# Attention with a gated MLP: weights normalized ahead of their transposes, the left keys of two heads in one product, gate tokens in pairs

## The chip, the cores and the metric

The kernel runs on one core of a Trainium2 chip. The metric is the device time of the whole program in microseconds (us). In the profile, PE is TensorE (matrix products; PEld its weight loads), DVE is VectorE, ACT is ScalarE, POOL is GpSimd and SP is SyncE, which issues the transfers.

## The reference

```python
q, k, v: (8, 12, 448, 64)              # batch, heads, tokens, head size
q_n = q / rms(q) * g_q;  k_n = k / rms(k) * g_k
scores = q_n @ k_n.T / 8
attn = exp(scores - max(scores));  attn = attn / (sum(attn) + 1e-9)
x = (attn @ v), heads side by side     # (8, 448, 768)
h = gelu_tanh(x @ w_in)                # w_in 768 x 1024
u, v = h[..., :512], h[..., 512:]
v_n = layernorm(v) * g_ln
v_s = w_sg @ v_n + b_sg                # w_sg 448 x 448, over the tokens
out = x + (u * v_s) @ w_out            # w_out 512 x 768
```

## The kernel before

448 is 3 x 128 + 64, so each head has three full tiles of tokens and 64 "left" tokens. The kernel works on pairs of heads, 48 in all (`i`), and on units of two pairs (`u`). Tokens are laid out so that the left tokens of the two pairs of a unit share one tile: a unit has seven score tiles, `C7 = 7`, and the middle one (`t == CM`, `CM = 3`) is shared.

Every number is carried as two half-precision parts, high and low (`h`, `l`), so that a product becomes three: high by high, high by low, low by high.

- `load_qk`, `squares`, `norms`, `split` fetch q and k, normalize them and transpose them by DMA into `qt`.
- `load_v`, `vsquares`, `vscale`, `vsplit` fetch v (three pairs at a time, tile `vr`, from a pool of two), find one power of two per batch and split v into `vh` and `vl`, of seven chunks of 64 columns.
- `scores(u)` makes for each of the seven tiles both heads' scores in a PSUM tile `s` of two banks (`ps_s` has two of them): products on TensorE (L389), the row maximum on VectorE (L392), two exponentials on ScalarE that also give the row sums (L394), then after a `yield` the split of the weights, not yet normalized, into two halves `ahl` (L397 ScalarE, L398 VectorE, 896 elements wide) and a DMA transpose into `at_all` (L403).
- `recips(i)` takes the reciprocal of the sums (GpSimd, VectorE), splits it in two (GpSimd), and spreads it over the 64 partitions of each head by 16 small products with `ident_h` (L423) into a PSUM tile; ScalarE copies that to `row` (L426).
- `pv(i)` calls `recips`, then runs 24 products of v with the transposed weights (L446): the left keys first, in 64x64 pieces, then the full chunks, 64 columns for each head side by side; it gives way (`yield`) after blocks 4 and 8. VectorE multiplies by `row` (L450), ScalarE and VectorE split the result into `xh`, `xl` (L453, L454).
- `moe(b)` is the MLP of one batch: the gate half of the first projection with tokens on the partitions (L510; left tokens L513, whose columns are halved), gelu, layer norm; the other half (L568); the gate over the tokens (L598: four accumulators `ms_`, one for each 128 columns `f`, 9 products over full token tiles and 3 over the left 64, at partitions 0 to 63 for `f` 0 and 1 and 64 to 127 for `f` 2 and 3); the product with `u` and its split (L603 to L608, on VectorE, GpSimd and ScalarE); and the second projection (L632 to L644), copied out by L648. Its accumulators come from `ps_m`, three PSUM banks.
- `weights()` decodes the MLP's weights, which arrive as double precision, in the first part of the run.

All of these are generators. The main loop goes over the pairs and takes steps from the streams `scores` (`SC = 7`), `pv` of the pair before (`SV = 4`), `weights`, and `moe` of the batch before (`M0` to `ML` steps a pair) in proportion to those numbers; the order in which they are written gives each instruction its priority. The framework's planner then sets the final order of each engine's instructions from the priorities and its own model of their times; each engine runs its instructions in that order.

Of the kernel before, what the change touches and what calls it, by code (L numbers as in the profile page):

```python
# [22 lines left out]


# [10 lines left out]
SC, SV = 7, 4  # L35
# [11 lines left out]
def kernel(  # L47
# [54 lines left out]
    ident_h = const.tile([P, P], F16, name="ident_h")  # L102
    A.activation(out=ident_h, in_=ident, func=AF.Copy)
# [180 lines left out]
    VR = {}  # L284

    def load_v(i):

        if i >= NI:  # L290
# [72 lines left out]
    def vsplit(i):  # L363
        r = R.setdefault(i, {})
        sc = VS[i // NP]["sc"]
        vh, vl = (att.tile([P, C7, D], F16, name="v" + c, bufs=NVH) for c in "hl")
        vr = VR.pop(i)
        vf = vh.rearrange("p c d -> p (c d)")
        A.activation(out=vf, in_=vr, func=AF.Copy, scale=sc)  # L369
        V.scalar_tensor_tensor(out=vl.rearrange("p c d -> p (c d)"), in0=vr, scalar=sc, in1=vf, op0=ALU.mult, op1=ALU.subtract)  # L370
        r.update(vh=vh, vl=vl)
# [3 lines left out]
    def scores(u):  # L375
# [3 lines left out]
        sums = sml.tile([P, C7, 2], F32, name="sums", bufs=2)  # L379
        U[u]["sums"] = sums  # L380
        for t in range(C7):
# [9 lines left out]
            nm = sml.tile([P, 2], F32, name="nm", bufs=6)  # L391
            V.tensor_reduce(out=nm, in_=ps[:, :, 0:S], axis=AX.X, op=ALU.max, negate=True)  # L392
            for h in range(2):
                A.activation(out=ps[:, h, 0:S], in_=ps[:, h, 0:S], func=AF.Exp, bias=nm[:, h:h + 1], accum_out=sums[:, t, h:h + 1])  # L394
            yield
            ahl = att.tile([P, 2, 2, S], F16, name="ahl", bufs=NAH)
            A.activation(out=ahl[:, 0], in_=ps[:, :, 0:S], func=AF.Copy)  # L397
            V.tensor_tensor(out=ahl[:, 1], in0=ps[:, :, 0:S], in1=ahl[:, 0], op=ALU.subtract)  # L398
# [7 lines left out]
    def recips(i):  # L406

        u, j = divmod(i, NG)
        cs = slice(0, C4) if j == 0 else slice(CM, C7)
        sums = U[u]["sums"][:, cs].rearrange("p t h -> p (t h)")  # L410
        x, y = (sml.tile([P, 2 * C4], F32, name=f"r{c}", bufs=2) for c in "xy")
        rh, rl = (sml.tile([P, 2 * C4], F16, name=f"r{c}", bufs=2) for c in "hl")
        G.tensor_scalar(out=x, in0=sums, scalar1=1e-9, scalar2=None, op0=ALU.add)  # L413
        V.reciprocal(out=y, in_=x)
        G.tensor_copy(out=rh, in_=y)  # L415
        G.tensor_tensor(out=rl, in0=y, in1=rh, op=ALU.subtract)
        ps = ps_v.tile([P, 512], F32, name="row", tag="pv")[:, 0:S]
        for n, t in enumerate(range(cs.start, cs.stop)):
            ks, o = (slice(0, P), t * P - j * S) if t != CM else ((lo, SM), (hi, 0))[j]
            for rx in (rh, rl):  # L420
                for h in range(2):
                    w = ks.stop - ks.start
                    mm(out=ps[h * HP:(h + 1) * HP, o:o + w], lhsT=rx[ks, 2 * n + h:2 * n + h + 1].broadcast_to([w, HP]),  # L423
                       rhs=ident_h[ks, ks], start=(n == 0 and rx is rh), stop=(n == CM and rx is rl), skip_group_check=True)
        row = att.tile([P, S], F32, name="row", bufs=1)
        A.activation(out=row, in_=ps, func=AF.Copy)  # L426
        return row

    XT = {}

    def pv(i):
# [3 lines left out]

        steps = [[(slice(0, P), c + h * C4) if c < CM else (slice(h * HP, (h + 1) * HP), CM) for h in range(2)]
                 for c in range(C4)]
        blocks = [(vx, n, hx) for vx, n in ((vh, 0), (vl, 0), (vh, C7)) for hx in steps]

        blocks = blocks[CM::C4] + [x for n, x in enumerate(blocks) if n % C4 != CM]  # L440
        row = recips(i)
        yield
        ps = ps_v.tile([P, 512], F32, name="pv")[:, 0:S]
        for k_, (vx, n, hx) in enumerate(blocks):
            for h, (ks, c) in enumerate(hx):
                mm(out=ps[h * HP:(h + 1) * HP], lhsT=vx[ks, c], rhs=at_all[ks, n + c, o:o + S],  # L446
                   start=(k_ == 0), stop=(k_ == len(blocks) - 1), skip_group_check=True)
            if k_ in (4, 8):
                yield
        V.tensor_tensor(out=ps, in0=ps, in1=row, op=ALU.mult)  # L450
        xh = xp.tile([P, S], F16, name="xh")
        xl = xp.tile([P, S], F16, name="xl")
        A.activation(out=xh, in_=ps, func=AF.Copy)  # L453
# [23 lines left out]
    def moe(b, early=False):  # L477
# [21 lines left out]
        for st, (t, g) in enumerate(steps):  # L499
# [20 lines left out]
            if st % 2 == 1:  # L520
# [60 lines left out]
        gl = []  # L581
# [7 lines left out]
        for f in range(FT):  # L589
            ps = ps_m.tile([P, 512], F32, name="ms_", tag="mm")  # L590
            n = 0
            for t in range(CK):
                p0, p1, o = 0, P, t * DH + f * P
                if t == CM:
                    p0 = f // 2 * HP
                    p1, o = p0 + HP, t * DH + f % 2 * P
                for vx, wx in ((vh, ws_h), (vh, ws_l), (vl, ws_h)):
                    mm(out=ps[:, 0:S], lhsT=vx[p0:p1, o:o + P], rhs=wx[p0:p1, t], start=(n == 0), stop=(n == 11))  # L598
                    n += 1
                if t == 1:  # L600
                    yield
            gt = mlp.tile([P, S], F32, name="gt", tag="gt", bufs=NOT)
            V.scalar_tensor_tensor(out=gt, in0=ps[:, 0:S], scalar=W["gw"][:, f:f + 1], in1=bb, op0=ALU.mult, op1=ALU.add)  # L603
            G.tensor_tensor(out=gt, in0=gt, in1=u[f], op=ALU.mult)  # L604
            A.activation(out=gh[:, f], in_=gt, func=AF.Copy)
            gl.append(mlp.tile([P, S], F32R, name="gl", tag="ug", bufs=5))
            G.tensor_tensor(out=gl[f], in0=gt, in1=gh[:, f].bitcast(F32), op=ALU.subtract)
            G.tensor_tensor(out=gtl[:, f, half], in0=gt[:, SM:S], in1=gh[:, f, SM:S].bitcast(F32), op=ALU.subtract)  # L608
# [183 lines left out]
```

## Time and profile before

| | |
|---|---|
| median of 3 runs | 1037.53 us (1032.77 to 1038.14) |
| the profiled execution | 1033.44 us |
| its span, first to last instruction | 1031.6 us |
| mean granted TensorE clock | 0.916 of full speed |
| moved by DMA | 155.70 MB |

A group's line gives the line of the kernel, engine, operation, what is written and read, how often, then busy us, the mean of one in ns, and the engine's idle time just before it with what ended it. A line of waits gives who waited, for whom, the total in us, how many times, and the longest. The rows of a stretch give its start and end, its length, and the busy time of PE, PEld, DVE, ACT and POOL with their instruction counts, then the granted clock, the share of the DMA engines and GB/s. For a product, `128*64` is the rows and columns of the array that it uses.

### The profile page before, as it was taken

The numbers are of one execution on the slowest core, as the hardware profiler recorded it, in microseconds if no ns is written. First come the engines' busy times: TensorE is split into PE (matmuls) and PEld (weight loads), VectorE is DVE, ScalarE is ACT, GpSimd is POOL, SyncE is SP. The second block draws the span as 40 slices with busy tenths as digits, with TensorE's granted clock in tenths as the row PEclk, the third lists the DMA queues.
The fourth block names the chain that finished last, engine by engine and source line by source line (L and its number), as shares of the span: only waits on it lengthen the run. The fifth ranks groups of instructions, "written<-read, shape, count | busy, mean of one in ns | idle before, by whom it ended". The sixth has DMA issues, their size and how long they took to land.

```text
span 1031.6 us, 16639 instructions
## 1 busy us (share of the span) xinstructions
PE 829.0 (80%) x5844; PEld 421.1 (41%) x5844; DVE 733.3 (71%) x1332; ACT 738.1 (72%) x1449; POOL 386.9 (38%) x403
## 2 busy tenths in 40 slices
PE   0243666858798997899689998999779998998798
PEld 0111222324444563346234553446324563454246
DVE  6698888999587667786677758786669666766230
ACT  3767779877868767777768767987777776877351
POOL 1468614567253505243251606341533414030021
PEclk9976687969899999999699998999889999999899
DMA  6998748776886398478886488959967676556102
GB/s 163 214 228 191 166 115 196 185 176 130 181 197 150 88 204 180 98 170 145 186 175 147 99 194 183 182 123 176 194 142 160 141 166 125 106 135 123 40 1 62
DMA packets 448004, 155.70 MB, mean 151 GB/s; under 512 B 404336, under 2 KB 441776, under 8 KB 447920
## 3 DMA queue, kind: packets, MB, share of 16 engines
q1 hardware_dynamic: 447344, 154.18, 69.0%
q8 instruction: 46, 0.75, 0.3%
q10 hardware_dynamic: 576, 0.46, 0.2%
q14 instruction: 38, 0.31, 0.1%
HBM read 43.57 MB, written 11.01 MB: 53 GB/s over the span
## 4 chain that ended last, share of the span: by engine, by line
PE 34%; DVE 21%; ACT 19%; DMA 11%; issue 8%; SPq 4%; POOL 4%; ACTq 0%; POOLq 0%; DVEq 0%
PE pv L446 6%; ACT s L394 5%; DVE ahl L398 5%; PE s L389 4%; DVE nm L392 3%; ACT ahl L397 2%; DMA vr<-in_v_dram 2%; ACT sqk L308 2%; DMA raw<-in_moe_w_in_dram 2%; DMA at<-ahl 2%; POOL qk L330 2%; DMA qt<-hl 2%; DMA qk<-in_k_dram 2%; ACT hl L334 2%; SPq L336 1%
## 5 line engine op out<-in xcount | busy, mean ns | idle before, releaser
L394 ACT ACTIVATE s<-s,nm 128x448 f32<-128x448 f32 x336 | 204.0, 607 | 109.8 <-DVE nm L392 106.8
L398 DVE TENSOR_TENSOR ahl<-s,ahl 128x896 f16<-128x896 f32 x168 | 182.1, 1085 | 100.8 <-ACT ahl L397 99.8
L389 PE MATMUL s<-qt 64*128 64x448 f16 (+1 forms) x1152 | 143.2, 390 | 110.7 <-DVE ahl L398 76.4
L392 DVE TENSOR_REDUCE nm<-s 128x2 f32<-128x896 f32 x168 | 180.8, 1082 | 40.5 <-PE s L389 40.0
L397 ACT ACTIVATE ahl<-s 128x896 f16<-128x896 f32 x168 | 153.4, 920 | 5.3 <-DMA at<-ahl 3.1
L446 PE MATMUL pv<-at,vh 128*64 128x448 f16 (+1 forms) x768 | 122.7, 398 | 16.4 <-DMA at<-ahl 7.6
L413 POOL TENSOR_SCALAR rx<-sums 128x8 f32<-128x8 f32 x48 | 13.4, 278 | 311.8 <-ACT s L394 310.4
L389 PEld LDWEIGHTS <-qt 64*128 64x128 f16 (+1 forms) x1152 | 45.3, 102 | 177.2 <-issue 135.9
L330 POOL TENSOR_TENSOR qk<-qk,ny 128x896 f32<-128x896 f32 x46 | 80.8, 1774 | 85.8 <-DVE ny L125 82.3
L335 POOL TENSOR_TENSOR hl<-qk,hl 128x896 f16<-128x896 f32 x46 | 87.7, 1917 | 55.1 <-ACT hl L334 54.5
L568 PEld LDWEIGHTS <-wi 128*128 128x128 f16 x576 | 55.9, 100 | 60.2 <-issue 14.1
L446 PEld LDWEIGHTS <-vh 128*64 128x64 f16 (+1 forms) x768 | 43.4, 117 | 84.3 <-issue 70.2
L309 DVE TENSOR_REDUCE ss<-sqk 128x14 f32<-128x896 f32 x48 | 51.8, 1080 | 29.2 <-ACT sqk L308 28.9
L394 ACT ACTIVATION_READ_ACCUMULATOR s<-s,nm 128x1 f32 x336 | 67.7, 201 | 0.0
L329 POOL TENSOR_TENSOR qk<-qk,gg 128x896 f32<-128x896 f32 x23 | 48.0, 2085 | 43.2 <-ACT sqk L308 39.3
L423 PE MATMUL row<-ident_h,rh 128*64 128x128 f16 (+1 forms) x384 | 36.7, 240 | 31.7 <-POOL rh L415 24.0
L604 POOL TENSOR_TENSOR gt<-gt,u 128x448 f32<-128x448 f32 x32 | 38.5, 1206 | 60.1 <-DVE gt L603 55.9
L446 PE MATMUL pv<-at,vl 128*64 128x448 f16 (+1 forms) x384 | 60.4, 394 | 0.0
L334 ACT ACTIVATE hl<-qk 128x896 f16<-128x896 f32 x48 | 44.9, 947 | 15.9 <-POOL qk L330 8.4
L308 ACT ACTIVATE sqk<-qk 128x896 f32<-128x896 f32 x48 | 45.6, 951 | 8.2 <-DVE ss L309 4.4
L510 PEld LDWEIGHTS <-xh 128*128 128x128 f16 x288 | 27.0, 101 | 49.2 <-issue 21.9
L369 ACT ACTIVATE vh<-vr,v_s 128x448 f16<-128x448 f32 x48 | 31.9, 668 | 19.7 <-PE pv L446 19.6
(996 smaller groups left out, 1960.8 us busy)
## 6 DMA issues: line engine op xcount, KB each, us to landing
out_dram<-ot SPq DMA_DIRECT2D x56, 192.0 KB, 2.9
vr<-in_v_dram SPq DMA_DIRECT2D x32, 192.0 KB, 3.3
raw<-in_moe_w_in_dram SPq DMA_DIRECT2D x12, 512.0 KB, 5.7
qk<-in_q_dram SPq DMA_DIRECT2D x47, 128.0 KB, 2.8
qk<-in_k_dram SPq DMA_DIRECT2D x47, 128.0 KB, 2.8
vr<-in_v_dram SPq DMA_DIRECT2D x32, 144.0 KB, 3.3
qk<-in_q_dram SPq DMA_DIRECT2D x47, 96.0 KB, 2.6
qk<-in_k_dram SPq DMA_DIRECT2D x47, 96.0 KB, 2.6
```

The source lines that it names most:

```text
L308: A.activation(out=skv, in_=U[u]["qk"][:, x].rearrange("p h c d -> p (h c) d"), func=AF.Square)
L309: V.tensor_reduce(out=SS[u][:, x], in_=skv, axis=AX.X, op=ALU.add)
L330: E.tensor_tensor(out=qk, in0=qk, in1=r["rs"][:, x * SSW:(x + 1) * SSW].unsqueeze(2).broadcast_to([P, SSW, D]), op=ALU.mult)
L334: A.activation(out=h_, in_=r["qk"][:, x], func=AF.Copy)
L335: E.tensor_tensor(out=l_, in0=r["qk"][:, x], in1=h_, op=ALU.subtract)
L389: mm(out=ps[r_, h, 0:S], lhsT=qt[hs, qx, t * P + r_.start:t * P + r_.stop], rhs=qt[hs, kx, j * S:(j + 1) * S], start=(m == 0), stop=(m == 2))
L392: V.tensor_reduce(out=nm, in_=ps[:, :, 0:S], axis=AX.X, op=ALU.max, negate=True)
L394: A.activation(out=ps[:, h, 0:S], in_=ps[:, h, 0:S], func=AF.Exp, bias=nm[:, h:h + 1], accum_out=sums[:, t, h:h + 1])
L397: A.activation(out=ahl[:, 0], in_=ps[:, :, 0:S], func=AF.Copy)
L398: V.tensor_tensor(out=ahl[:, 1], in0=ps[:, :, 0:S], in1=ahl[:, 0], op=ALU.subtract)
L446: mm(out=ps[h * HP:(h + 1) * HP], lhsT=vx[ks, c], rhs=at_all[ks, n + c, o:o + S], start=(k_ == 0), stop=(k_ == len(blocks) - 1), skip_grou ...
L568: done = mm(out=ps[:, 0:S], lhsT=ww[:, g, f * P:(f + 1) * P], rhs=xx, start=(n == 0), stop=(n == 17))
```

## The change

The reciprocal of the row sums is taken in `scores`, from each tile's own sums, and the weights are multiplied by it (and by 1024, `WSC`, to use the half-precision range) while they are split, one head at a time. `recips`, `row`, `ident_h` and the multiply in `pv` go; `xh` and `xl` take 1/1024 in. v gets an eighth chunk: the left keys of the first head lie in chunk 3 (other half zero), those of the second in chunk 4 (other half zero), so that one product of 128 columns serves both heads; the zeros are written once, into two `vr` tiles that are now allocated by hand. `pv` is one block without a `yield` inside. In `moe`, the left tokens of the first projection are one step, and the gate runs `f` in pairs (0, 2) and (1, 3) with the left tokens of both side by side.

```diff
+WSC = 2.0 ** 10
-SC, SV = 7, 4
+SC, SV = 7, 3
...
-    ident_h = const.tile([P, P], F16, name="ident_h")
-    A.activation(out=ident_h, in_=ident, func=AF.Copy)
...
+    C8 = C7 + 1
+    vr_all = [ld.tile([P, GV, C8, D], F32, name=f"vr{n}", bufs=1) for n in range(NVR)]
+    for x in vr_all:
+        G.memset(x[hi, :, CM], 0.0)
+        G.memset(x[lo, :, C4], 0.0)
...
-        vr = ld.tile([P, GV, C7, D], F32, name="vr", bufs=NVR)
+        vr = vr_all[i // GV % NVR]
...
-        vh, vl = (att.tile([P, C7, D], F16, name="v" + c, bufs=NVH) for c in "hl")
+        vh, vl = (att.tile([P, C8, D], F16, name="v" + c, bufs=NVH) for c in "hl")
...
-            nm = sml.tile([P, 2], F32, name="nm", bufs=6)
+            nm, sums = (sml.tile([P, 2], F32, name=c, bufs=6) for c in ("nm", "sums"))
             V.tensor_reduce(out=nm, in_=ps[:, :, 0:S], axis=AX.X, op=ALU.max, negate=True)
             for h in range(2):
-                A.activation(..., func=AF.Exp, bias=nm[:, h:h + 1], accum_out=sums[:, t, h:h + 1])
+                A.activation(..., func=AF.Exp, bias=nm[:, h:h + 1], accum_out=sums[:, h:h + 1])
+            rc = sml.tile([P, 2], F32, name="rc", bufs=6)
+            V.tensor_scalar(out=sums, in0=sums, scalar1=1e-9, scalar2=1.0 / WSC, op0=ALU.add, op1=ALU.mult)
+            V.reciprocal(out=rc, in_=sums)
             yield
             ahl = att.tile([P, 2, 2, S], F16, name="ahl", bufs=NAH)
-            A.activation(out=ahl[:, 0], in_=ps[:, :, 0:S], func=AF.Copy)
-            V.tensor_tensor(out=ahl[:, 1], in0=ps[:, :, 0:S], in1=ahl[:, 0], op=ALU.subtract)
+            for h in range(2):
+                A.activation(out=ahl[:, 0, h], in_=ps[:, h, 0:S], func=AF.Copy, scale=rc[:, h:h + 1])
+                V.scalar_tensor_tensor(out=ahl[:, 1, h], in0=ps[:, h, 0:S], scalar=rc[:, h:h + 1], in1=ahl[:, 0, h],
+                                       op0=ALU.mult, op1=ALU.subtract)
...
-    def recips(i):
-        ...
...
     def pv(i):
-        blocks = blocks[CM::C4] + [x for n, x in enumerate(blocks) if n % C4 != CM]
-        row = recips(i)
-        yield
-        ...
-            if k_ in (4, 8):
-                yield
-        V.tensor_tensor(out=ps, in0=ps, in1=row, op=ALU.mult)
+        parts = ((vh, 0), (vl, 0), (vh, C7))
+        for k_, (vx, n) in enumerate(parts):
+            mm(out=ps, lhsT=vx[:, CM:CM + 2].rearrange("p c d -> p (c d)"), rhs=at_all[:, n + CM, o:o + S],
+               start=(k_ == 0), stop=False, skip_group_check=True)
+        for c in range(CM):
+            for vx, n in parts:
+                for h in range(2):
+                    mm(out=ps[h * HP:(h + 1) * HP], lhsT=vx[:, c + h * (C4 + 1)], rhs=at_all[:, n + c + h * C4, o:o + S],
+                       start=False, stop=(c == CM - 1 and n == C7), skip_group_check=True)
-        A.activation(out=xh, in_=ps, func=AF.Copy)
-        V.tensor_tensor(out=xl, in0=ps, in1=xh, op=ALU.subtract)
+        A.activation(out=xh, in_=ps, func=AF.Copy, scale=1.0 / WSC)
+        V.scalar_tensor_tensor(out=xl, in0=ps, scalar=1.0 / WSC, in1=xh, op0=ALU.mult, op1=ALU.subtract)
         XT[i] = (xh, xl)
         del R[i]
+        yield
...
-            if st % 2 == 1:
+            if st % 2 == 1 and (early or t != CM or g == NP - 1):
                 yield
...
-        for f in range(FT):
-            ps = ps_m.tile([P, 512], F32, name="ms_", tag="mm")
-            ...
+        for f0 in range(2):
+            psf = {f: ps_m.tile([P, 512], F32, name="ms_", tag="mm") for f in (f0, f0 + 2)}
+            for f, ps in psf.items():
+                ...
+                yield
+            for n, (vx, wx) in enumerate(((vh, ws_h), (vh, ws_l), (vl, ws_h))):
+                for f, ps in psf.items():
+                    p0, o = f // 2 * HP, CM * DH + f0 * P
+                    mm(out=ps[:, 0:S], lhsT=vx[p0:p0 + HP, o:o + P], rhs=wx[p0:p0 + HP, CM], start=False, stop=(n == 2))
+            for f, ps in psf.items():
+                ...
             yield
```

More of the change, by code (lines that the diff above doesn't have):

```diff
@@ L292, in load_v @@
         b, g = divmod(i, NP)
-        vr = ld.tile([P, GV, C7, D], F32, name="vr", bufs=NVR)
+        vr = vr_all[i // GV % NVR]
         vp = vr.rearrange("p g c d -> p g (c d)")
         src = v[b, 2 * g:2 * (g + GV)].rearrange("(g h) (p c) d -> h p g (c d)", h=2, c=C7)
-        for h, half, s0, c0, n in ((0, lo, 0, 0, C4), (0, hi, 0, C4, CM), (1, lo, C4, C4, CM), (1, hi, CM, 0, C4)):
+        for h, half, s0, c0, n in ((0, lo, 0, 0, C4), (0, hi, 0, C4, CM), (1, lo, C4 + 1, C4, CM), (1, hi, C4, 0, C4)):
             nc.sync.dma_start(out=vp[half, :, s0 * D:(s0 + n) * D], in_=src[h][:, :, c0 * D:(c0 + n) * D])
@@ L349, in vsquares @@
             VS["part", b] = sml.tile([P, NP // GV], F32, name="vpart", bufs=2)
-        n = GV * C7 * D
+        n = GV * C8 * D
         sk = prep.tile([P, n], BF16, name="sqv", tag="t4", bufs=HLB)
@@ L378, in scores @@
         qt = U[u]["qt"]
-        sums = sml.tile([P, C7, 2], F32, name="sums", bufs=2)
-        U[u]["sums"] = sums
         for t in range(C7):
@@ L390, in scores @@
                            rhs=qt[hs, kx, j * S:(j + 1) * S], start=(m == 0), stop=(m == 2))
-            nm = sml.tile([P, 2], F32, name="nm", bufs=6)
+            nm, sums = (sml.tile([P, 2], F32, name=c, bufs=6) for c in ("nm", "sums"))
             V.tensor_reduce(out=nm, in_=ps[:, :, 0:S], axis=AX.X, op=ALU.max, negate=True)
             for h in range(2):
-                A.activation(out=ps[:, h, 0:S], in_=ps[:, h, 0:S], func=AF.Exp, bias=nm[:, h:h + 1], accum_out=sums[:, t, h:h + 1])
+                A.activation(out=ps[:, h, 0:S], in_=ps[:, h, 0:S], func=AF.Exp, bias=nm[:, h:h + 1], accum_out=sums[:, h:h + 1])
+            rc = sml.tile([P, 2], F32, name="rc", bufs=6)
+            V.tensor_scalar(out=sums, in0=sums, scalar1=1e-9, scalar2=1.0 / WSC, op0=ALU.add, op1=ALU.mult)
+            V.reciprocal(out=rc, in_=sums)
             yield
             ahl = att.tile([P, 2, 2, S], F16, name="ahl", bufs=NAH)
-            A.activation(out=ahl[:, 0], in_=ps[:, :, 0:S], func=AF.Copy)
-            V.tensor_tensor(out=ahl[:, 1], in0=ps[:, :, 0:S], in1=ahl[:, 0], op=ALU.subtract)
+            for h in range(2):
+                A.activation(out=ahl[:, 0, h], in_=ps[:, h, 0:S], func=AF.Copy, scale=rc[:, h:h + 1])
+                V.scalar_tensor_tensor(out=ahl[:, 1, h], in0=ps[:, h, 0:S], scalar=rc[:, h:h + 1], in1=ahl[:, 0, h],
+                                       op0=ALU.mult, op1=ALU.subtract)
             src = ahl.rearrange("p x h n -> p (x h n)")
@@ L404, in scores @@
             yield
-    def recips(i):
[L408 to L427, printed above, removed]
     XT = {}
@@ L580, in moe @@
         gh = mlp.tile([P, FT, S], F32R, name="gh", tag="vggh")
-        gl = []
+        gl = {}
         vh, vl = V2["vh"], V2["vl"]
@@ L588, in moe @@
         bb = W["bb"]
-        for f in range(FT):
-            ps = ps_m.tile([P, 512], F32, name="ms_", tag="mm")
[L591 to L608, printed above, removed]
@@ new lines, in moe @@
+        for f0 in range(2):
+            psf = {f: ps_m.tile([P, 512], F32, name="ms_", tag="mm") for f in (f0, f0 + 2)}
+            for f, ps in psf.items():
+                n = 0
+                for t in range(CM):
+                    o = t * DH + f * P
+                    for vx, wx in ((vh, ws_h), (vh, ws_l), (vl, ws_h)):
+                        mm(out=ps[:, 0:S], lhsT=vx[:, o:o + P], rhs=wx[:, t], start=(n == 0), stop=False)
+                        n += 1
+                yield
[4 more added lines that the diff above has]
+            for f, ps in psf.items():
+                gt = mlp.tile([P, S], F32, name="gt", tag="gt", bufs=NOT)
+                V.scalar_tensor_tensor(out=gt, in0=ps[:, 0:S], scalar=W["gw"][:, f:f + 1], in1=bb, op0=ALU.mult, op1=ALU.add)
+                G.tensor_tensor(out=gt, in0=gt, in1=u[f], op=ALU.mult)
+                A.activation(out=gh[:, f], in_=gt, func=AF.Copy)
+                gl[f] = mlp.tile([P, S], F32R, name="gl", tag="ug", bufs=5)
+                G.tensor_tensor(out=gl[f], in0=gt, in1=gh[:, f].bitcast(F32), op=ALU.subtract)
+                G.tensor_tensor(out=gtl[:, f, half], in0=gt[:, SM:S], in1=gh[:, f, SM:S].bitcast(F32), op=ALU.subtract)
```

7 lines of the change are left out of this document (removed).

## The prediction

> **What bounds the kernel now.** I read the page first, then the stretches by engine, then the chain of waits, the waits of each engine, the groups by line, and last TensorE's timeline where the change touches it.
>
> Busy time on the page:
> ```profile
> span 1031.6 us, 16639 instructions
> PE 829.0 (80%) x5844; PEld 421.1 (41%) x5844; DVE 733.3 (71%) x1332; ACT 738.1 (72%) x1449; POOL 386.9 (38%) x403
> ```
> The span cut in three, and three single stretches (us; then PE, PEld, DVE, ACT, POOL busy; granted clock; DMA):
> ```profile
> 0.00:300.00 300.00, 171.50 (x1162) 79.66 (x1163) 248.33 (x435) 217.85 (x424) 152.10 (x136) 0.82 0.78 178
> 300.00:900.00 600.00, 541.85 (x3908) 276.36 (x3905) 434.39 (x817) 454.52 (x901) 211.86 (x231) 0.95 0.73 155
> 900.00:1032.00 132.00, 115.64 (x780) 65.10 (x777) 50.53 (x82) 65.71 (x126) 22.92 (x36) 0.95 0.33 72
> ...
> 100.00:200.00 100.00, 67.00 (x425) 27.88 (x425) 87.99 (x166) 84.43 (x158) 42.85 (x37) 0.74 0.74 168
> 700.00:800.00 100.00, 83.59 (x604) 40.50 (x601) 73.89 (x136) 75.13 (x150) 32.56 (x32) 0.91 0.86 171
> 800.00:900.00 100.00, 96.43 (x714) 51.60 (x714) 66.84 (x130) 74.80 (x153) 27.25 (x37) 1.00 0.64 137
> ```
> No engine is full throughout. Up to 300 us VectorE leads (83%; 88% between 100 and 200), from 300 us on TensorE (90%). The chain of waits, whole span by engine and the 300 to 900 stretch by line:
> ```profile
> PE 34%; DVE 21%; ACT 19%; DMA 11%; issue 8%; SPq 4%; POOL 4%; ACTq 0%; POOLq 0%; DVEq 0%
> ...
> by line: PE pv L446 7.0%; ACT s L394 6.9%; issue 6.7%; DVE ahl L398 4.9%; PE s L389 4.6%; DVE nm L392 3.6%; ACT ahl L397 2.7%; ACT sqk L308 2.3%; DMA vr<-in_v_dram 2.3%; ACT hl L334 2.2%; DMA qt<-hl 2.0%; DMA at<-ahl 1.9%; PE row L423 1.5%;
> ```
> So the end is set by three engines handing work to each other. A microsecond of an engine lies on that chain with a weight of its chain share over its busy share: PE 34/80 = 0.425, DVE 21/71 = 0.296, ACT 19/72 = 0.264. I price by these weights; they assume that the mixture stays, which the rivals drop. Waits from 300 to 900 us:
> ```profile
> PE s L389 <- DVE ahl L398: 18.1, 18, 3.0
> PE row L423 <- POOL rh L415: 12.9, 7, 5.3
> ...
> DVE ahl L398 <- ACT ahl L397: 69.0, 58, 3.8
> ...
> ACT s L394 <- DVE nm L392: 69.2, 39, 6.0
> ```
> VectorE and ScalarE wait mostly for one another inside a score tile; TensorE, when it waits, waits for a score tile's subtraction or for the reciprocals.
>
> **The change part by part.** Durations by group (busy us, mean ns, idle before), then two single lines:
> ```profile
> L394 ACT ACTIVATE s<-s,nm 128x448 f32<-128x448 f32 x336 | 204.0, 607 | 109.8 <-DVE nm L392 106.8
> L398 DVE TENSOR_TENSOR ahl<-s,ahl 128x896 f16<-128x896 f32 x168 | 182.1, 1085 | 100.8 <-ACT ahl L397 99.8
> ...
> L397 ACT ACTIVATE ahl<-s 128x896 f16<-128x896 f32 x168 | 153.4, 920 | 5.3 <-DMA at<-ahl 3.1
> ...
> L394 ACT ACTIVATION_READ_ACCUMULATOR s<-s,nm 128x1 f32 x336 | 67.7, 201 | 0.0
> ...
> L607 POOL TENSOR_TENSOR gl<-gt,gh 128x448 fp32r<-128x448 f32 x32 | 36.8, 1150 | 7.9 <-ACT gh L605 7.8
> ...
> L370 DVE SCALAR_TENSOR_TENSOR vl<-vr,v_s,vh 128x448 f16<-128x448 f32 x48 | 36.6, 764 | 3.0 <-ACT vh L369 3.0
> ...
> L450 DVE TENSOR_TENSOR pv<-pv,row 128x448 f32<-128x448 f32 x48 | 30.0, 624 | 22.3 <-PE pv L446 22.0 <-PE mo__6671 L636 0.4
> ...
> L426 ACT ACTIVATE row<-row 128x448 f32<-128x448 f32 x48 | 26.0, 542 | 6.5 <-PE row L423 6.3
> ...
> L453 ACT ACTIVATE xh<-pv 128x448 f16<-128x448 f32 x48 | 25.9, 540 | 18.4 <-DVE pv L450 18.4
> ...
> L414 DVE RECIPROCAL ry<-rx 128x8 f32<-128x8 f32 x48 | 9.4, 196 | 15.8 <-POOL rx L413 15.5
> ...
> L135 DVE TENSOR_SCALAR v_x<-v_x x8: 135/144/155, 38.6 to 849.5; 128x1 f32<-128x1 f32 x8
> ...
> L603 DVE SCALAR_TENSOR_TENSOR gt<-ms__3456,gw,bb x1: 684/684/684, 343.5 to 343.5; 128x448 f32<-128x448 f32 x1
> ```
> TensorE's row products (L423), in the three stretches:
> ```profile
> 0.00:300.00 300.00, 12.11 (x192) 8.24 (x192) 0.82 0.78 178
> 300.00:900.00 600.00, 26.18 (x512) 18.00 (x512) 0.95 0.73 155
> 900.00:1032.00 132.00, 3.09 (x64) 2.12 (x64) 0.95 0.33 72
> ```
> At 16 products a head pair these are 12, 32 and 4 pairs, so 42, 112 and 14 score tiles (3.5 a pair).
>
> Its timeline (start, us; both at clock 1.0), first a run of whole products, then where forms alternate, a split `pv`, and the gate's left tokens:
> ```profile
> 654.30 0.38 PE L510 MATMUL mv__7104<-wi,xl 128*128 128x512 f16 x1
> 654.52 0.59 PE L510 MATMUL mv__7104<-wi,xh 128*128 128x512 f16 x2
> ...
> 519.67 0.39 PE L510 MATMUL mv__5655<-wi,xh 128*128 128x512 f16 x1
> 520.00 0.30 PE L513 MATMUL mv__5575<-wi,xh 128*64 128x256 f16 x1
> ...
> 337.36 0.85 PE L446 MATMUL pv<-at,vh 64*64 64x448 f16 x6
> 338.15 0.74 PE L389 MATMUL s<-qt 64*128 64x448 f16 x6
> 338.82 0.38 PE L446 MATMUL pv<-at,vh 128*64 128x448 f16 x2
> ...
> 341.41 0.35 PE L598 MATMUL ms__3456<-ws_h,vl 128*128 128x448 f16 x1
> 341.60 0.35 PE L598 MATMUL ms__3491<-ws_h,vh 128*128 128x448 f16 x1
> 341.89 0.36 PE L598 MATMUL ms__3456<-ws_h,vh 64*128 64x448 f16 x1
> ```
> A 512-wide product takes 0.22 us from start to start, 0.33 when the next has another form (rows*columns); a 448-wide one 0.19 and 0.29. A change of form costs 0.10 us.
>
> The sum for 300 to 900 us:
> 1. Row products go: 1.5% of the chain, −9.0 (bounds 0 and the whole 26.2).
> 2. TensorE's waits for `rh` go: 12.9 x 0.425 = −5.5.
> 3. The multiply by `row` and `recips`' reciprocal go from VectorE: 32 x (0.624 + 0.196) = 26.2, x 0.296 = −7.8. The copy of `row` goes from ScalarE: 32 x 0.542 = 17.3, x 0.264 = −4.6. Three GpSimd steps a pair go; off the path, counted at nothing: GpSimd is 38% busy.
> 4. `pv` in one block: if one foreign block fewer splits it, two changes, 32 x 0.2 x 0.425 = −2.7 (bounds 0 and double). The whole product of the left keys replaces a pair that ran side by side, so it frees no stream of columns: nothing.
> 5. First projection: left-token products no longer handed out two at a time; up to 12 changes a batch, 5.5 batches, 6.6 x 0.425 = −2.8 (0 if the planner still mixes them).
> 6. Gate: a batch's left tokens take 4 x (3 x 0.19 + 0.2) = 3.1 us, in pairs 2 x 0.77 = 1.5: 5.5 x 1.5 x 0.425 = −3.6. The pairs hold two of three `ps_m` buffers; the 9 products of the next accumulator (1.7 us) cover an evacuation of 0.684, and without that cover each waits 0.7.
> 7. VectorE per tile: two halves with a per-row scalar, nearest L603, 2 x 0.68 − 1.085 = +0.27, and two tiny operations, 0.144 + 0.196 = +0.34: 0.61 x 112 = 68.3, x 0.296 = +20.2. L398's own 4.9% of the chain gives 29.4 x 0.61/1.085 = 16.5. I take +18.4.
> 8. ScalarE per tile: two halves, between L453's 0.540 and L394's 0.607, taken 0.56: +0.20 x 112 x 0.264 = +5.9.
> 9. But the subtraction can begin after half a copy, 0.36 earlier, at the 58 waits of 69.0 us: 20.9 x 0.296 = −6.2 (0 if the waits are for something earlier).
> 10. Two more hand-overs a tile (sums to VectorE, reciprocal to ScalarE). No row prices one; between 0 and a tiny operation's 0.144, taken 0.1: 112 x 0.1 x 0.296 = +3.3.
> 11. `v` has eight chunks, not seven: at most 0.764 x 64/448 = 0.11 on each of VectorE and ScalarE, 32 x 0.11 x 0.56 = +2.0. `ident_h` and the zero fill of `vr` fall into the start and cost nothing while the first loads run; without that, under 1 us.
>
> Sum −12.6. The transposes on SyncE's queue become ready with the second half, some 0.3 us later, and loads queue behind them; `at<-ahl` has 1.9% of the chain, so I count it within 10.
>
> 0 to 300 us: rows 12.1 x 0.425 = −5.1, the waits for `rh`, taken as half of the later stretch's, −2.8, `pv` and gate −1. VectorE: 42 x 0.61 − 12 x 0.82 = +15.8 in a stretch where it leads; between its weight (+4.7) and all (+15.8) I take +7. Sum −1.9. 900 us on, TensorE 88% busy and mostly alone: rows −2, gate of two batches −2, VectorE +1.6, and at the end the second pair's two gate chains come together on GpSimd (one more 1.15 and its neighbour, +2): −0.4.
>
> Together −14.9 us: span 1031.6 to 1016.7. The profiled execution took 1033.4, so 1.8 lies around the span: 1018.5. The median of the runs, 1037.5, stands 4 us above that execution; I give 1018.
>
> **The rivals.**
> *Slower: VectorE's queue.* The tiny operations wait for the second exponential's sum. If one stands in VectorE's order before another tile's maximum, that maximum waits up to 0.607 + 0.201 = 0.81 us, and ScalarE (which waited 69.2 us for maxima) with it. It eats the gain from 15/0.81 = 19 of 168 tiles on; at a quarter of them, 42, it ends 34 us above the forecast, 1052. For it: VectorE at 88% between 100 and 200 us. Against: the waits now are handed between two tiles in flight, so the planner can put other work there.
>
> *TensorE was the bound alone.* Then 300 to 900 us shrinks until VectorE is the limit: 434.4 + 68.3 − 26.2 + 3.5 = 480, at the 88% of the 100 to 200 row 545 us, −55, and 975 in all. For it: 96.43 of 100 in the row from 800. Against: TensorE has only 34% of the chain.
>
> *The clock takes it back.* The row from 700 shows 83.6% busy and clock 0.91, that from 800 shows 96.4% and 1.00. TensorE after has some 542 − 26 − 13 − 8 = 495 of 587 us, 84%: at 0.91 for 0.95 its work grows by 4.4%, 21.8 x 0.425 = +9, 1027. The Trainium skill (TensorE: Matmul & The Clock Gate, Why this matters for your kernels) advises against idle gaps of over some 3 us between bursts, since the clock falls; the rows agree in direction, not in which gap does it.
>
> *No change: work only moved.* The three engines' sum from 300 to 900 us is 1430.8; after, TensorE −47, VectorE +46, ScalarE +9. At the same overlap the time stays 1033. The same if the planner does not set the pairs side by side. The Trainium skill (TensorEngine Tiling (Array Packing), PSUM Bottleneck) says packing speeds TensorE but not the evacuation of PSUM, which can become the limit.
>
> **How the numbers follow.** Forecast 0.46 (1000 to 1028), TensorE alone 0.12, clock 0.14, no change 0.09, slower 0.19. From 985 to 1043 leaves out about half of the second and half of the last, 0.16 in all. A difference of 0.5% is about what can be told here. Faster: 0.46 + 0.12 + 0.09 of the clock's = 0.67; same: 0.05 + 0.09 = 0.14; slower 0.19.
>
> **What would show it.** Right: PE's busy time near 765, DVE's near 800, no row products, shorter waits of DVE for `ahl` copies, 0.19 us between the gate's left pairs. Wrong: ScalarE's copy idle for a reciprocal for more than some 20 us in all, VectorE waiting for exponentials before a tiny operation, or a clock under 0.90 with TensorE idle as before.

## The result, and the profile after

The changed kernel takes 1168.95 us (median of 4 runs, 1168.50 to 1171.91) where the kernel before takes 1036.42 on the same chip (median of 4, 1032.77 to 1038.14): a ratio of 1.129 (95% interval 1.125 to 1.133), 133 us slower. The forecast was 1018. The profiled execution took 1171.91 us, at a mean granted clock of 0.846 where before had 0.916. One execution further down, of `halves_turn`, ran slow, at a clock of 0.645 and 1282.98 us, and is left out of what is compared.

Span and busy time of the changed kernel, from its page:
```profile
span 1170.1 us, 15089 instructions
PE 820.3 (70%) x4932; PEld 404.1 (35%) x4932; DVE 807.6 (69%) x1740; ACT 780.7 (67%) x1568; POOL 352.0 (30%) x263
```
912 products are gone, and yet every engine has a smaller share of the span than before. So no engine became full; the engines stand idle for one another more. The same three stretches (the last row ends with the longer span):
```profile
0.00:300.00 300.00, 140.23 (x769) 61.77 (x769) 231.05 (x475) 198.56 (x392) 128.74 (x97) 0.78 0.68 156
300.00:900.00 600.00, 461.14 (x2816) 225.45 (x2816) 431.18 (x951) 423.70 (x855) 174.31 (x120) 0.86 0.62 138
900.00:1170.00 270.00, 218.96 (x1348) 116.91 (x1347) 145.35 (x315) 158.41 (x323) 49.00 (x46) 0.89 0.44 97
```
From 300 to 900 us TensorE was 90% busy before and is 77% now; VectorE, at 72%, is where it was. The groups around a score tile (busy us, mean ns, idle before and its cause):
```profile
L405 DVE SCALAR_TENSOR_TENSOR ahl<-s,rc,ahl 128x448 f16<-128x448 f32 x336 | 225.5, 679 | 122.7 <-ACT ahl L404 121.2
L392 PE MATMUL s<-qt 64*128 64x448 f16 (+1 forms) x1152 | 149.8, 405 | 198.4 <-DVE ahl L405 172.9
L404 ACT ACTIVATE ahl<-s,rc 128x448 f16<-128x448 f32 x336 | 208.6, 632 | 110.8 <-DVE ahl L405 57.3
L397 ACT ACTIVATE s<-s,nm 128x448 f32<-128x448 f32 x336 | 203.5, 606 | 110.6 <-DVE nm L395 107.0
L399 DVE TENSOR_SCALAR sums<-sums 128x2 f32<-128x2 f32 x168 | 45.9, 273 | 62.3 <-ACT s L397 61.7
```
The waits over the whole span, before and then after (who waits, for whom, us, times, longest):
```profile
PE s L389 <- DVE ahl L398: 76.4, 35, 9.0
PE pv L446 <- DMA at<-ahl: 7.6, 3, 3.0
PE row L423 <- DVE xl L454: 2.7, 1, 2.7
...
DVE ahl L398 <- ACT ahl L397: 99.8, 82, 4.5
...
ACT s L394 <- DVE nm L392: 106.8, 58, 6.0
```
```profile
PE s L392 <- DVE ahl L405: 172.9, 59, 11.9
PE pv L423 <- DMA at<-ahl: 46.4, 14, 8.3
...
DVE ahl L405 <- ACT ahl L404: 121.2, 151, 3.9
DVE sums L399 <- ACT s L397: 61.7, 72, 2.2
...
ACT s L397 <- DVE nm L395: 107.0, 102, 5.3
ACT ahl L404 <- DVE ahl L405: 57.3, 64, 2.5
```
The chain of waits of this execution can be followed back only from the end to 1098 us, so the argument goes by waits and single tiles. The wait that grew most is TensorE's for a score tile's PSUM to come free: 76.4 to 172.9 us. The last line has no counterpart before: ScalarE, which copies a tile's weights, waits for VectorE, which subtracts them. One tile shows it, before and then after (start, us, engine, operation, idle before and its releaser):
```profile
960.53 0.21 ACT L394 ACTIVATION_READ_ACCUMULATOR s<-s,nm 128x1 f32 x1
960.77 0.92 ACT L397 ACTIVATE ahl<-s 128x896 f16<-128x896 f32 x1
961.72 1.09 DVE L398 TENSOR_TENSOR ahl<-s,ahl 128x896 f16<-128x896 f32 x1 [0.42 <-ACT ahl L397]
```
```profile
559.89 0.17 DVE L399 TENSOR_SCALAR sums<-sums 128x2 f32<-128x2 f32 x1 [0.96 <-ACT s L397]
560.10 0.17 DVE L400 RECIPROCAL rc<-sums 128x2 f32<-128x2 f32 x1
560.35 0.64 ACT L404 ACTIVATE ahl<-s,rc 128x448 f16<-128x448 f32 x1 [0.48 <-ACT s L397]
561.01 0.68 DVE L405 SCALAR_TENSOR_TENSOR ahl<-s,rc,ahl 128x448 f16<-128x448 f32 x1 [0.75 <-ACT ahl L404]
561.62 1.08 DVE L395 TENSOR_REDUCE nm<-s 128x2 f32<-128x896 f32 x1
561.74 0.63 ACT L404 ACTIVATE ahl<-s,rc 128x448 f16<-128x448 f32 x1 [0.75 <-DVE ahl L405]
562.61 0.68 DVE L405 SCALAR_TENSOR_TENSOR ahl<-s,rc,ahl 128x448 f16<-128x448 f32 x1
```
Before, copy and subtraction take 2.04 us from the copy's start (960.77 to 962.81). After, they go by turns: copy of head 0, subtraction of head 0, copy of head 1, subtraction of head 1. The second copy starts only when the first subtraction ends (561.69), although it reads other columns; so it does in 158 of the 168 tiles, taken in order of time. VectorE fills the pause with the next tile's maximum, and the last subtraction waits until that is done: 2.94 us (560.35 to 563.29). Two small operations and two hand-overs stand ahead of all this.

**The hold of a score tile.** There are two PSUM tiles `s`. I took, in each trace, the time from the first product of each of the 168 tiles to the end of its last subtraction (the hold) and from there to the first product of the tile that takes its place (the gap). With two tiles used in turn, half the mean of their sum is the time from one tile to the next by construction; what the table can show is which part grew:

| | hold | gap | half the sum | tile to tile, measured |
|---|---|---|---|---|
| before | 9.62 | 1.53 | 5.58 | 5.60 |
| after | 10.99 | 1.83 | 6.41 | 6.41 |

The difference, 0.83 (of the unrounded means) x 168 = 139 us, is the loss with 6 us to spare, and most of it is hold: 1.37 us more a tile, against 0.30 of gap. That the hold also sets the pace doesn't follow from the sum. In `two_psum_before` below, where TensorE is 99% busy, the same account over both heads' tiles gives 10.19 and 0.30, half the sum 5.24, and 5.27 measured. For the changed kernel it rests on TensorE's longer waits above and on the runs below, which alter what happens inside the hold. Two parts of the hold grew: from the end of the exponentials to the copy's start, 0.85 to 1.63 (1.03 to the reciprocal, 0.60 on to the copy), and from the copy's start to the last subtraction's end, 2.53 to 4.05. Two shrank, perhaps since engines were freer: products to maximum, 2.57 to 2.15, and maximum to exponential, 1.03 to 0.54.

### The profile page after: what moved, and what is told of

It is laid out like the page before. It is cut to its first block, busy times and chain, and to the rows that moved or that the text cites. A ratio compares the mean times of both kernels' runs of the same rounds, so it can differ in the third digit from the quotient of the medians.

```text
span 1170.1 us, 15089 instructions
## 1 busy us (share of the span) xinstructions
PE 820.3 (70%) x4932; PEld 404.1 (35%) x4932; DVE 807.6 (69%) x1740; ACT 780.7 (67%) x1568; POOL 352.0 (30%) x263
## 5 line engine op out<-in xcount | busy, mean ns | idle before, releaser
L405 DVE SCALAR_TENSOR_TENSOR ahl<-s,rc,ahl 128x448 f16<-128x448 f32 x336 | 225.5, 679 | 122.7 <-ACT ahl L404 121.2
L392 PE MATMUL s<-qt 64*128 64x448 f16 (+1 forms) x1152 | 149.8, 405 | 198.4 <-DVE ahl L405 172.9
L404 ACT ACTIVATE ahl<-s,rc 128x448 f16<-128x448 f32 x336 | 208.6, 632 | 110.8 <-DVE ahl L405 57.3
L428 PE MATMUL pv<-at,vh 128*64 128x448 f16 x576 | 110.1, 441 | 0.0
L399 DVE TENSOR_SCALAR sums<-sums 128x2 f32<-128x2 f32 x168 | 45.9, 273 | 62.3 <-ACT s L397 61.7
L423 PE MATMUL pv<-at,vh 128*128 128x448 f16 x96 | 42.4, 441 | 63.8 <-DMA at<-ahl 46.4
L428 PE MATMUL pv<-at,vl 128*64 128x448 f16 x288 | 63.2, 436 | 0.0
L428 PEld LDWEIGHTS <-vh 128*64 128x64 f16 x576 | 39.2, 133 | 55.6 <-issue 45.0
L433 DVE SCALAR_TENSOR_TENSOR xl<-pv,xh 128x448 f16<-128x448 f32 x48 | 29.7, 619 | 31.9 <-ACT xh L432 31.9
L432 ACT ACTIVATE xh<-pv 128x448 f16<-128x448 f32 x48 | 26.0, 542 | 32.5 <-PE pv L428 32.4
```

The costliest lines, as they stand in the source:

```text
L392: mm(out=ps[r_, h, 0:S], lhsT=qt[hs, qx, t * P + r_.start:t * P + r_.stop], rhs=qt[hs, kx, j * S:(j + 1) * S], start=(m == 0), stop=(m == 2))
L399: V.tensor_scalar(out=sums, in0=sums, scalar1=1e-9, scalar2=1.0 / WSC, op0=ALU.add, op1=ALU.mult)
L404: A.activation(out=ahl[:, 0, h], in_=ps[:, h, 0:S], func=AF.Copy, scale=rc[:, h:h + 1])
L405: V.scalar_tensor_tensor(out=ahl[:, 1, h], in0=ps[:, h, 0:S], scalar=rc[:, h:h + 1], in1=ahl[:, 0, h], op0=ALU.mult, op1=ALU.subtract)
L428: mm(out=ps[h * HP:(h + 1) * HP], lhsT=vx[:, c + h * (C4 + 1)], rhs=at_all[:, n + c + h * C4, o:o + S], start=False, stop=(c == CM - 1 and ...
```

## The experiments

Theory: the turns of the two engines on one PSUM tile, and the reciprocal ahead of the copy, lengthen the hold. Rivals: VectorE's wait for the sums alone; the clock; the rest of the change (one-block `pv`, MLP). All differences below are to the kernel before in the same set of runs, 1033.81, 1036.11, 1036.72 or 1037.20 us.

**Half the change each.** `norm_alone` is the kernel before with the weights normalized in `scores` as in the change; `pv`'s blocks, its split left keys and the MLP stay as before.
```diff
+ scores as in the change (sums, rc, scaled halves by turns)
- row = recips(i);  ps = ps * row
```


> The kernel before with one part of the change: the reciprocal of each tile's sums in scores, the weights scaled while they are split one head at a time, no row products. pv in its old blocks, gate and projection as before. Theory 1 (the two heads' halves take turns: the second copy on ScalarE stands behind the first subtraction on VectorE, and the tiny operations make VectorE wait): nearly all of the 133 us is here, 1130 to 1180 us. Rival 2 (pv in one block and the eighth chunk of v set TensorE waiting): within 20 us of before, 1020 to 1055. Rival 3 (both in equal parts): near 1100.

1164.41 us, 1.125 (1.121 to 1.130): +131.

`rest_alone` is the changed kernel with `recips`, `row` and the 896-wide copy and subtraction put back.

> The changed kernel with the old normalization put back: whole-tile copy and subtraction, reciprocals and row products after the sums of all tiles, multiply by row. pv in one block, eighth chunk of v, gate in pairs and the projection's left tokens in one step stay. Theory 1 (halves in turns): near the kernel before or a little faster, 1015 to 1045. Rival 2 (pv in one block, v's scale): 1120 to 1170. Rival 3 (both): near 1100.

1045.70 us, 1.011 (1.007 to 1.014): +12. The two add up to 143, the whole change makes 133. Nearly all of the loss comes with the normalization.

**The turns.** `halves_turn` takes the kernel before and only cuts its copy and subtraction in two, without scaling:
```diff
-            A.activation(out=ahl[:, 0], in_=ps[:, :, 0:S], func=AF.Copy)
-            V.tensor_tensor(out=ahl[:, 1], in0=ps[:, :, 0:S], in1=ahl[:, 0], op=ALU.subtract)
+            for h in range(2):
+                A.activation(out=ahl[:, 0, h], in_=ps[:, h, 0:S], func=AF.Copy)
+                V.tensor_tensor(out=ahl[:, 1, h], in0=ps[:, h, 0:S], in1=ahl[:, 0, h], op=ALU.subtract)
```


> The kernel before with one edit: copy and subtraction of a tile are split in two, copy of head 0, its subtraction, copy of head 1, its subtraction, with no scaling and no reciprocals per tile. Only the turns and the two extra instructions are added. Theory 1 (the turns cost): 1090 to 1140. Rival 1b (what costs is the tiny operations' wait for the sums): only the added busy time, 168 x 0.14 us on VectorE and 168 x 0.16 us on ScalarE, of which a third shows: 1040 to 1060.

1121.17 us, one execution and so without an interval: +87. Hold and gap are 10.43 and 1.78, 6.12 from tile to tile. Its waits:
```profile
DVE ahl L399 <- ACT ahl L398: 150.4, 145, 4.2
...
ACT ahl L398 <- DVE ahl L399: 43.7, 58, 3.0
...
PE s L389 <- DVE ahl L399: 65.9, 36, 7.8
```
The wait of the copy for the subtraction is there without any reciprocal. `halves_first` differs from it in order alone:
```diff
             for h in range(2):
                 A.activation(out=ahl[:, 0, h], in_=ps[:, h, 0:S], func=AF.Copy)
+            for h in range(2):
                 V.tensor_tensor(out=ahl[:, 1, h], in0=ps[:, h, 0:S], in1=ahl[:, 0, h], op=ALU.subtract)
```


> The kernel before with copy and subtraction of a tile in two halves, no scaling, both copies written ahead of both subtractions. Against the run with the halves in turns (1121) only the order differs. Theory 1 (turns): most of the 88 us goes, 1045 to 1075. Rival (two more instructions a tile cost by themselves): 1100 or more.

1040.70 us, 1.005 (1.001 to 1.010): +5, hold 9.59. So twice the instructions cost 5 us, the order the other 83.

`copies_first` does the same reordering in the changed kernel.

> The changed kernel with one edit: both ScalarE copies of a tile are written ahead of both VectorE subtractions, so that the second copy does not stand behind the first subtraction; three hand-overs between the engines become one. Theory 1 (the turns are the cost): a good part comes back; a tile's tail falls from some 2.9 us to 2.5, with less waiting on both engines, 1070 to 1130. Rival 1b (VectorE waiting for the sums, and its added work): at most 20 us come back, 1150 or more. Rival 2 (pv in one block): no change, 1160 to 1175.

1131.02 us, 1.093 (1.089 to 1.097): +97, so 35 of the 133 us come back, hold 10.78. A tile of it:
```profile
562.84 1.16 ACT L404 ACTIVATE ahl<-s,rc 128x448 f16<-128x448 f32 x2 [0.49 <-ACT s L397]
564.03 1.27 DVE L406 SCALAR_TENSOR_TENSOR ahl<-s,rc,ahl 128x448 f16<-128x448 f32 x2 [0.94 <-ACT ahl L404]
```
The first subtraction needs head 0's copy alone, which ends after half of the 1.16, but it starts after both, here and in all 168 tiles. In this order too an operation on one half waits for the other engine's latest one on the other half. The halves share the tile `ahl` as well as `s`, and no run tells which of the two makes the wait in this order; for the order by turns `two_psum_before` below does, as it divides `s` alone.

**The reciprocal ahead of the copy.** `whole_scaled` is the changed kernel with copy and subtraction 896 wide again, both heads scaled by head 0's reciprocal (so head 1 is not normalized by its own sums).
```diff
+            A.activation(out=ahl[:, 0], in_=ps[:, :, 0:S], func=AF.Copy, scale=rc[:, 0:1])
+            V.scalar_tensor_tensor(out=ahl[:, 1], in0=ps[:, :, 0:S], scalar=rc[:, 0:1], in1=ahl[:, 0], ...)
```


> The changed kernel with copy and subtraction of a score tile again 896 wide, one instruction each, both heads scaled by head 0's reciprocal; what it leaves out is head 1's own scale. The reciprocals stay between the exponentials and the copy. Theory 1 (turns of halves cost some 90 us, the reciprocals the rest): 1070 to 1095. If the turns were all: 1030 to 1050. If the reciprocals on the way were nearly all: 1110 or more.

1123.26 us, 1.086 (1.080 to 1.090): +87. Set against `rest_alone` (each to its own before) normalizing ahead of the copy costs 87 - 12 = 75 us without any turns. That is a net figure: with the scale the copy takes 1006 ns for 918 and the subtraction 1147 for 1085, and the work of `recips` is gone. Most of what is added stands ahead of the copy: from the end of the exponentials to its start a tile takes 2.21 us, 0.93 in `rest_alone`. Its waits:
```profile
PE s L392 <- DVE ahl L404: 142.6, 57, 11.9
...
DVE sums L399 <- ACT s L397: 59.6, 66, 2.2
```
`tiny_only` adds the two small operations to the kernel before, and nothing uses their result.
```diff
+            V.tensor_scalar(out=sx, in0=sums[:, t], scalar1=1e-9, scalar2=2.0 ** -10, op0=ALU.add, op1=ALU.mult)
+            V.reciprocal(out=rc, in_=sx)
```


> The kernel before plus the two tiny VectorE operations of each tile (sum scaled, reciprocal), whose results nothing uses; ScalarE's copy does not wait for them. They still stand in VectorE's order and wait for the second exponential's sum. Measured of them in the changed kernel: 0.27 and 0.16 us busy and 62 us of waiting. If VectorE's own wait and work are the cost of the reciprocals: 1060 to 1085. If it is ScalarE that waits for the reciprocal: under 1050.

1061.01 us, 1.025 (1.021 to 1.030): +25.
```profile
PE s L389 <- DVE ahl L401: 105.5, 41, 11.4
...
DVE sx L396 <- ACT s L394: 54.3, 72, 2.6
```
VectorE's wait for the sums (54.3 us, 72 times) is nearly as long as in the changed kernel (61.7, 72), and it costs a fifth of the loss. That rival by itself falls; the larger part of the 75 us comes only when copy and subtraction use the result. The copy is not held back here: 0.82 us from the end of the exponentials, 0.85 before.

`no_ts` leaves one of the two small operations out: no `tensor_scalar`, `WSC` 1 and no 1e-9 added to the sums.

> The changed kernel without the first of the two tiny operations: the reciprocal is taken of the bare sum; left out are the 1e-9 and the factor 1024 (1/1024 at the end becomes 1). It takes 0.27 us and one hand-over on the way of every score tile. If the time follows how long a score tile holds its PSUM banks (two tiles, so half of each microsecond of a tile's life, 168 times): 0.45 x 168 / 2 = 38 us less, 1120 to 1140. If the weights of the prediction hold (46 us of VectorE at 0.3): 14 us less, 1150 to 1160.

1145.71 us, 1.105 (1.102 to 1.107): 24 us less than the change's +133, between what a hold lengthened by its full duration and what the chain weights of the prediction would give. Its trace shows why the full price is not reached: the way from the exponentials to the copy is 0.32 us shorter (1.63 to 1.30), but the hold only 0.14 (to 10.86), since other parts of it grew, and the gap 0.15.

**A PSUM tile for each head.** `two_psum` is the changed kernel with the two banks of `s` as two tiles; the maximum becomes two operations of 448 columns.
```diff
-            ps = ps_s.tile([P, 2, 512], F32, name="s")
+            ps = [ps_s.tile([P, 512], F32, name=f"s{h}") for h in range(2)]
...
-            V.tensor_reduce(out=nm, in_=ps[:, :, 0:S], ...)
+            for h in range(2):
+                V.tensor_reduce(out=nm[:, h:h + 1], in_=ps[h][:, 0:S], ...)
```


> The changed kernel with a PSUM tile of its own for each head's scores instead of one tile of two banks, in the written order copy, subtraction, copy, subtraction; the maximum becomes two reductions of 448. The built program's second copy then carries no wait for VectorE. If the order between the two engines comes from sharing one PSUM tile, the waits of ScalarE's copy for VectorE's subtraction (57 us) go, and the time falls at least as with both copies first, 1080 to 1131; if the two extra reductions (168 x 0.15 us) eat it, 1131 to 1150.

1056.58 us, 1.021 (1.017 to 1.025): 112 of the 133 us come back, with the reciprocals still there.
```profile
PE s L392 <- DVE ahl L406: 97.5, 44, 12.7
...
DVE ahl L406 <- ACT ahl L405: 34.3, 60, 1.3
DVE sums L400 <- ACT s L398: 35.7, 47, 1.9
```
VectorE's wait for the copy falls from 121.2 to 34.3 us, as the tile of its own lets each subtraction follow its own copy. `two_psum_before` does it in the kernel before, with the halves by turns of `halves_turn`.

> The kernel before with a PSUM tile of its own for each head's scores, two maxima of 448 in place of one of 896, and copy and subtraction in halves by turns, no scaling. Against the run with the same turns in one shared tile (1121) only the tile is split. If the shared tile makes the order: back to 1025 to 1050. If a bank that comes free by itself is worth something beyond that (the products of head 0 can start while head 1's bank is still read): under 1030, faster than before. If the turns cost by themselves: 1100 or more.

**993.06 us, 0.958 (0.956 to 0.960)**: 44 us faster than the kernel before, so the order that cost 83 us on a shared tile is no loss here. `halves_first`, also free of turns, has +5. How much of the difference comes from halves that follow one another and how much from banks that come free one at a time was not separated.
```profile
span 989.9 us, 17152 instructions
PE 870.9 (88%) x5844; PEld 431.9 (44%) x5844; DVE 745.2 (75%) x1668; ACT 741.6 (75%) x1617; POOL 389.1 (39%) x403
```
```profile
300.00:900.00 600.00, 591.47 (x4139) 292.80 (x4138) 469.58 (x1091) 488.97 (x1086) 221.92 (x245) 0.99 0.76 163
```
```profile
PE s L389 <- DVE ahl L400: 43.6, 25, 7.4
```
From 300 to 900 us TensorE is 99% busy at a clock of 0.99: this version is bound by TensorE there, as neither kernel was. `two_psum_norm` puts the change's normalization on top of the split tile (`norm_alone` with a tile for each head).

> The kernel before with the normalization alone (pv in its old blocks, old MLP), and a PSUM tile for each head. Against the same with one shared tile (1164) and against halves without normalization in split tiles (993). If the reciprocal on the way costs as much as with a shared tile (some 85 us from the run with whole-width copies): 1070 or more. If the shared tile was most of the price: 1020 to 1050, 30 to 55 us over 993, of which the tiny operations' wait and work alone were 25.

1058.69 us, 1.021 (1.016 to 1.027): 22 - (-44) = 65 us more than without it, with no turns to pay.
```profile
PE s L390 <- DVE ahl L404: 85.7, 33, 13.5
...
DVE sums L398 <- ACT s L396: 39.2, 59, 1.5
```
So normalizing ahead of the copy costs 65 to 75 us net without any turns, on a shared tile and on split ones, the dearer copies and subtractions included.

**The rest of the change.** `pv_only` has the eighth chunk, the whole product, `vr` by hand and one block for `pv`, with old normalization and old MLP.

> The kernel before with v's eighth chunk, the whole product of the left keys, hand-allocated vr tiles and pv in one block (3 steps a pair), old normalization and old MLP. The two together with the MLP's part measured 12 us above before. The prediction's term 4 gives -3 and term 11 +2: 1032 to 1036. If pv as one block holds up TensorE for the score tiles: 1040 to 1055.

1054.64 us, 1.017 (1.013 to 1.021): +18. `pv_block` only takes the `yield`s out of the kernel before, `recips` within the same step, and sets `SV = 3`.
```diff
-            if k_ in (4, 8):
-                yield
```


> The kernel before with pv, its row products included, written as one step without giving way inside, 3 steps a pair; v's chunks, the left keys' 64x64 pieces and all else as before. The whole pv part measured 1054.6. If the block holds up TensorE: 1045 to 1060. If the cost comes from the eighth chunk and the hand-allocated vr tiles (later loads of v, one more chunk on two engines): 1030 to 1040.

1054.37 us, 1.019 (1.015 to 1.022): +17. So the loss is the block's, with the `SV = 3` that both runs have and that was not tried alone; eighth chunk and whole product together come to nothing.
```profile
PE row L423 <- DVE xl L451: 18.2, 3, 11.1
PE pv L445 <- DMA at<-ahl: 18.0, 8, 3.8
...
DVE pv L447 <- PE pv L445: 33.8, 19, 8.4
```
Before, these three stood at 2.7, 7.6 and 22.0 us: TensorE waits within the block, for the PSUM of the pair before and for the transposes, and VectorE for its last product. That this is for want of a place to give way is what the waits suggest.

`moe_only` is the kernel before with the change's MLP (gate in pairs, left tokens of the projection in one step).

> The kernel before with the MLP's part of the change alone: gate accumulators in pairs with the left tokens side by side, left tokens of the first projection as one step. The prediction's terms 5 and 6 give -6.4 us from 300 to 900 and -2 after: 1026 to 1030. If the pairs' grip on two of three accumulators costs more than the products save: 1040 to 1050.

1028.56 us, 0.991 (0.989 to 0.994): -8.2. And on top of the best version, `two_psum_moe`:

> The two edits that gained, together: a PSUM tile for each head with copy and subtraction in halves, no normalization ahead of the transposes, and the MLP's gate in pairs with the projection's left tokens in one step. Separately they gave -43.7 and -8.2 us. If both act on TensorE's free time: 980 to 990. If the score tiles no longer bound the time and TensorE's products do, the second may count more: under 980.

995.01 us, 0.961 (0.957 to 0.964), which cannot be told from 993.06 without it. I don't know why these 8 us are not to be had there. TensorE's busy time is the same, 869.6 and 870.9, where `moe_only` lowered it from 829.0 to 811.9, and the clock is lower in each of the four runs, 0.935 to 0.940 against 0.944 to 0.948.

## Why the prediction was wrong, point by point

**The step that failed first is 9.** "But the subtraction can begin after half a copy, 0.36 earlier": it does, and the second copy then waits for that subtraction. Taken as -6.2 (0 at the other end), it measured +87 by itself (`halves_turn`), 83 of it for the order. The turns were in no term and no rival, because I took the two halves of `s` for independent; the runs show that for the program's order of waits the tile is one thing.

**Steps 7, 8 and 10 took the wrong measure.** The durations were near: halves of 0.68 forecast and 679 ns measured, VectorE busy near 800 forecast and 807.6 measured, ScalarE's halves 0.56 forecast and 632 ns measured. But a microsecond was priced at 0.26 to 0.30, its engine's share of the chain of waits. The added work lies between the exponentials and the release of the tile, on a resource of which there are two, and every microsecond of hold costs 168/2 = 84 us of the run unless another part of the hold or the gap shrinks. Term 10, the two hand-overs, stood at +3.3; the end of the exponentials to the copy's start grew by 0.78 a tile, 66 us by that measure. That this is near the 75 and 65 us of the runs is partly chance: in `whole_scaled` the same part grew by 1.28 over `rest_alone`, 107 us by that measure, and the cost was 75. `tensor_scalar` has a median of 169 ns but a mean of 273:
```profile
L399 DVE TENSOR_SCALAR sums<-sums x168: 136/169/1880, 27.7 to 1098.3; 128x2 f32<-128x2 f32 x168
```
That the added work falls into a long hold could be read in the trace of before: 9.62 of the 11.16 us from one use of a tile to the next. How much of it would show could not, since TensorE waited for score tiles for only 18.1 of the 600 us from 300 on.

Turns (87) and reciprocal (75) do not add to the 121 that the normalization costs on top of `rest_alone`'s 12: they overlap. Why by so much was not tried; a copy that is late for one reason may have less to wait for the other.

**Step 4 had the wrong sign.** `pv` in one block was -2.7, between 0 and double; it is +17. The term counted the changes of form that a split brings and left out the waits inside a block that nothing may interrupt, which the lines of `pv_block` show.

**Steps 5 and 6 met the number, but their mechanism only in part**: -2.8 - 3.6, and 2 us more in the last stretch, together -8.4; `moe_only` measured -8.2. Step 5 is seen in that run: the projection's 288 products for left tokens stand in 41 unbroken rows, 73 before. Step 6 hardly is: 12 of the gate's 48 pairs of left products start side by side, and from start to start the 96 take 19.3 us, 20.8 before, not half. In the changed kernel neither came about: 80 rows, and no pair side by side, as the two accumulators of a pair come to their left tokens 1.9 to 7.4 us apart. The planner set the order, as the prediction's rival of no change had allowed. First the changed kernel, then `moe_only`:
```profile
388.63 0.36 PE L583 MATMUL ms__3378<-ws_h,vh 64*128 64x448 f16 x1
...
391.11 0.36 PE L583 MATMUL ms__3379<-ws_h,vh 64*128 64x448 f16 x1
```
```profile
234.63 0.36 PE L603 MATMUL ms__2181<-ws_h,vh 64*128 64x448 f16 x1
234.63 0.36 PE L603 MATMUL ms__2182<-ws_h,vh 64*128 64x448 f16 x1
```
So -8.2 beside -8.4 is partly luck, and the changed kernel did not get either term as it was meant. Step 11 was small as taken: `pv_only` and `pv_block` agree to 1 us.

**Steps 1 to 3**, what goes with `recips`, can't be read off any run, as no kernel here drops it without putting something in its place.

**The rivals.** The slower one named a wait that is there (VectorE for the exponentials' sums: 61.7/72 = 0.86 us each, forecast 0.81; 72 tiles, forecast 42). As the whole cause it falls with `tiny_only`, 25 us. "TensorE was the bound alone" was wrong for this change, though TensorE did become the bound from 300 to 900 us once each head had its tile (`two_psum_before`). The clock fell, 0.916 to 0.846, and TensorE's busy time is 820.3 where 765 was forecast, with 912 products fewer. The clock goes roughly with TensorE's busy share here: with the same 5844 products 0.948 at 88% (`two_psum_before`), 0.916 at 80% (before) and 0.879 at 77% (`halves_turn`), and 0.846 at the changed kernel's 70%; `two_psum`, 0.900 at 83%, does not fit. Which of the two moves the other, no run shows. The direction agrees with the Trainium skill (TensorE: Matmul & The Clock Gate, Why this matters for your kernels), which advises against long idle gaps; the waits for a score tile now last up to 11.9 us, 9.0 before. What share of the 133 us the clock then adds was not separated. The Trainium skill (TensorEngine Tiling (Array Packing), PSUM Bottleneck) says that packing speeds up TensorE but not the emptying of PSUM, which may then become the limit. Here emptying did, TensorE's waits for it going from 76.4 to 172.9 us, but because it was made longer and not because TensorE was faster, and through waits and not through a full engine.

Of the signs that were to show the forecast right, VectorE's busy time and the missing row products came. TensorE's busy time, a shorter wait for the copies (99.8 us before, 121.2 after) and the gate's pairs did not.

## What to carry to other kernels

Ask of each PSUM tile how long it is held, from first write to last read, and who waits for its release. Where an engine does, an edit inside the hold can cost up to its full length times the tiles over the buffers (here 84 us for each microsecond), whatever its engine's share of a chain; how much of that other parts of the hold take back has to be measured (`no_ts`: 24 us of a forecast 38). Cutting one operation into halves on a tile that two engines share can put them into turns; a tile for each half turned the same edit from 87 us lost into 44 us won. And a block that may give way is worth something even when each of its breaks costs.

## What was not expected of the hardware

- Two operations of 448 columns are busy for longer than one of 896, but not twice as long: in `halves_first` two copies take 2 x 549 = 1098 ns where one took 920, and two subtractions 2 x 617 = 1234 where one took 1085. The run is only 0.5% longer.
- Operations on 128x2 elements vary tenfold: 136 to 1880 ns for the `tensor_scalar`. One of the long ones, with GpSimd at work from 587.94:
```profile
587.94 3.34 POOL L335 TENSOR_TENSOR qk<-qk,ny 128x896 f32<-128x896 f32 x2 [3.33 <-DVE ny L125]
...
588.78 0.88 DVE L399 TENSOR_SCALAR sums<-sums 128x2 f32<-128x2 f32 x1
```
All 30 that took over 300 ns overlap an operation of GpSimd, and of the 121 that overlap none the longest took 172 ns. The reciprocal behind it, of the same 128x2 elements, overlaps GpSimd 31 times and never took over 168. Why the one is held up and the other isn't, no run here tested.
